# Leading small matmuls, wider fillers, masks through an ACT copy, and a re-searched order in an attention and mixer kernel

## The chip, the cores and the metric

The kernel runs on one core of a Trainium2 chip. The metric is the device time of one execution in microseconds (us), median of several executions; lower is better. The profile's span is 1.7 us shorter than the device time of the same execution (170.1 against 171.84 in the profile of the kernel before), so the two are compared only with their own kind. Engines are called PE (matmuls), DVE (vector), ACT (scalar), POOL and SP.

## The reference

A gated recurrent attention of 4 batches, 8 heads, 768 positions, head size 48, then a token mixer and a channel mixer.

```python
# attention, per batch and head
for t in range(S):
    state = alpha[t][:, None] * state + outer(k[t], v[t])
    y[t] = q[t] @ state
x = y.transpose(0, 2, 1, 3).reshape(B, S, H * D)        # (4, 768, 384)
# mixer
h  = relu(x^T @ w_tok1) @ w_tok2                        # 768 -> 256 -> 768
u  = x + h^T
h2 = relu(u @ w_ch1) @ w_ch2                            # 384 -> 1536 -> 384
return u + h2                                           # fp32
```

## The kernel before

The kernel cuts the positions of each batch into three groups of 256, twelve groups in all; groups 0 to 2 are batch 0. For each group it forms cumulated gates ("cum"), their exponentials, scaled keys and queries ("kk", "qq"), transposes of both ("trk", "trq", evicted by "evk", "evq"), the scores of two halves ("G0", "G1"), their causal masks ("mask0", "mask1"), the state updates (the K product "K", additions "sa", multiplications "sm"), the output of the group itself ("y"), and two rounds of matmuls that add the state's part ("ia", "ib", with a small copy between them as a fence). Evictions "x" then give the mixer its input.

Three properties matter here.

First, every engine works its instructions in the order of a long list, found by a search that ran against a small model of the chip. A token such as `G0_2t` means scores of half 0 of group 2 on PE; a token that ends in `n` is left out.

```python
ENGINES = {"t": "PE", "s": "ACT", "v": "DVE", "g": "POOL", "y": "SP", "n": "NONE"}
ORDER = """
f2cumw_0n f1trq_1t f1trq_0t f2cumw_1t f1trk_1n f1trk_0n ...
... K1t E2s G0_1t mask0_1v IE2s ldw_wt10g Et2s y0t ia0t
f2y_2n fe0s f2trk_2t ib0t f1trk_2t x0_0s f2G0_2n x1_0s ld_qt2y qq2g trq2t ld_kt2y f0trk_2t kk2v sa0_1v sm0_1g
ld_vt2y trk2t f0y_1t y1t ldw_wt20g evk2v evq2s sa1_1v sm1_1g f0G0_2t G0_2t mask0_2v ld_at3y f1K_2t f0G1_2t vb2s
ia1t K2t sa0_2v G1_2t P3g sm0_2g ldw_wc10g t1_0_1_0t ... mask1_2v cum3t E3s ib1t ... y2t ia2t x0_1v fe2v ib2t ...
"""                                                      # ... marks cuts
```

Second, PE's granted clock falls to half in places. In the profile of the kernel before it is 0.50 from 23.34 to 26.75 us, 3.41 us, behind a wait of PE of 1.58 us. The model has a rule of its own for this clock. Against the half clock the list holds optional fillers, matmuls on a zero tile into a PSUM bank that is about to be used:

```python
def fill(nm, bank, sizes=(1, 2, 4)):                     # groups 0 to 2 only
    return [O(f"f{j}{nm}_", {"PE": pe([384] * z)["PE"], "NONE": (0.0, 0.0)}, -100, writes=[bank],
              mm=z, emit=lambda e, z=z: g.fill(bank, z)) for j, z in enumerate(sizes)]
```

Third, the model takes PE's instructions to come in blocks, and lets PE wait where a block is late. The profile of before shows 19 packets of 16 KB on PE's instruction queue for 2461 matmuls and as many weight loads, and one wait of PE for issue, behind matmul 351; that such a wait is one for a block is the model's assumption. The place where it lets one block end and the next begin is called an edge here. The model counts matmuls (two instructions each), asks for the next block when it crosses an edge, and expects it `fetch(s)` ns later:

```python
count, edge, fetched = 0.0, 95.0, 0.0
...
while edge < count + o.mm:
    cross = st + occ * (edge - count) / o.mm
    late = max(0.0, fetched - cross)
    occ, lat = occ + late, lat + late
    fetched = cross + late + fetch(st)
    edge += 127.5

def fetch(s):
    return 4300.0 if s < 20000.0 else 5000.0 if s < 60000.0 else 4300.0 if s < 82000.0 else 3300.0
```

A mask multiplies 1024 scores per partition, read from PSUM in f32, by a bf16 triangle, and writes bf16:

```python
masks.append(O(f"mask{sl}_", dve(1024), 12 + sl, writes=[gtm], reads=[gp], preds=[G],
               emit=lambda e, sl=sl, gp=gp: g.mask(gtm, gp, sl)))
```

## Time and profile before

| what | kernel before |
|---|---|
| device time, median of the first 3 timed runs | 170.48 us (170.17 to 170.59) |
| the profiled execution | 171.84 us, span 170.1 us, mean clock 0.99 |
| PE busy | 163.0 us, 96% of the span |
| half clock inside the work | 23.3 to 26.8 us |
| hand-over: end of the second state matmuls of group 2 | 28.45 us |
| saturated stretch: hand-over to the start of the last matmul | 138.18 us |
| tail after it | 3.49 us |

The last three rows add up to the span: 28.45 + 138.18 + 3.49 = 170.12 us. I use this cut throughout: before the hand-over PE waits for loads and for batch 0's attention, after it PE is never short of work. The list of what PE waited for says how short the first part's list of suspects is (the columns are microseconds in total, number of times, longest):

```profile
PE ps L675 <- issue: 1.6, 1, 1.6
PE ps L675 <- DVE zs L604: 1.1, 1, 1.1
```

The second line is the start of the kernel. The first is a wait for nothing but the instruction itself, and it is the only one of its kind.

### The profile page before, as it was taken

The numbers are of one execution on the slowest core, as the hardware profiler recorded it, in microseconds if no ns is written. First come the engines' busy times: TensorE is split into PE (matmuls) and PEld (weight loads), VectorE is DVE, ScalarE is ACT, GpSimd is POOL, SyncE is SP. The second block draws the span as 40 slices with busy tenths as digits, with TensorE's granted clock in tenths as the row PEclk, the third lists the DMA queues.
The fourth block names the chain that finished last, engine by engine and source line by source line (L and its number), as shares of the span: only waits on it lengthen the run. The fifth ranks groups of instructions, "written<-read, shape, count | busy, mean of one in ns | idle before, by whom it ended". The sixth has DMA issues, their size and how long they took to land.

```text
span 170.1 us, 5655 instructions
## 1 busy us (share of the span) xinstructions
PE 163.0 (96%) x2461; PEld 104.5 (61%) x2461; DVE 118.3 (70%) x209; ACT 81.8 (48%) x160; POOL 60.2 (35%) x69
## 2 busy tenths in 40 slices
PE   7899969999999999999999999999999999999992
PEld 3476635676666666666666766766665666665661
DVE  4279837787869778989798897898653647573151
ACT  3868644755884637278637651666412313141000
POOL 5047637430830132929869939600200000000000
PEclk9999978999999999999999999999999999999999
DMA  5999999999999386999949200010003000110343
GB/s 137 322 321 320 228 248 294 229 271 270 252 216 286 103 227 204 323 329 258 291 152 272 101 2 0 4 50 4 0 4 139 0 4 2 46 46 4 115 177 125
DMA packets 57369, 27.10 MB, mean 159 GB/s; under 512 B 50432, under 2 KB 57344, under 8 KB 57344
## 3 DMA queue, kind: packets, MB, share of 16 engines
q1 hardware_dynamic: 53232, 23.34, 48.6%
q0 software_dynamic: 3824, 3.15, 11.9%
q8 instruction: 19, 0.31, 0.7%
q10 hardware_dynamic: 288, 0.26, 0.4%
q14 instruction: 6, 0.05, 0.1%
HBM read 25.17 MB, written 4.72 MB: 176 GB/s over the span
## 4 chain that ended last, share of the span: by engine, by line
PE 92%; DMA 2%; DVE 2%; issue 1%; ACT 1%; DVEq 0%
PE ps L889 28%; PE ps L894 28%; PE ps L675 18%; PE ps L870 5%; PE ps L863 4%; PE ps L737 3%; PE ps L881 2%; DMA at<-in_alpha_dram 2%; PE ps L741 2%; PE ps L868 1%; DVE pkk L722 1%; DVE pkq L722 1%; ACT la L669 1%; ACT IE L706 0%; DVE x L779 0%
## 5 line engine op out<-in xcount | busy, mean ns | idle before, releaser
L894 PE MATMUL ps<-wc,rt 128*128 128x384 bf16 (+2 forms) x300 | 52.3, 320 | 0.0
L889 PE MATMUL ps<-ut,wc 128*128 128x384 bf16 x288 | 51.5, 326 | 0.0
L858 ACT ACTIVATE rt<-ps 128x384 bf16<-128x384 f32 x55 | 25.7, 492 | 30.4 <-PE ps L889 30.2
L894 PEld LDWEIGHTS <-rt 128*128 128x128 bf16 x300 | 27.8, 98 | 16.4
L889 PEld LDWEIGHTS <-wc 128*128 128x128 bf16 x288 | 27.1, 98 | 17.1
L791 DVE TENSOR_TENSOR gtm<-ps,mk 128x1024 bf16<-128x1024 f32 x24 | 28.7, 1217 | 3.1 <-PE ps L675 2.7
L860 DVE TENSOR_SCALAR rt<-ps 128x384 bf16<-128x384 f32 x41 | 21.5, 550 | 6.0 <-PE ps L889 5.9
L898 DVE TENSOR_TENSOR o<-ps,u 128x384 f32<-128x384 f32 (+2 forms) x25 | 13.2, 535 | 11.1 <-PE ps L894 9.1
L820 POOL TENSOR_TENSOR ss<-tmp,E 128x192 bf16<-128x192 f32 x13 | 6.6, 507 | 26.6 <-DVE tmp L817 26.1
L722 POOL TENSOR_TENSOR pkq<-qt,E 128x768 bf16<-128x768 f32 x7 | 12.7, 1813 | 6.2 <-PE ps L863 5.2
L675 PE MATMUL ps<-zs 128*128 128x384 bf16 x50 | 12.8, 382 | 1.1 <-DVE zs L604 1.1
L722 POOL TENSOR_TENSOR pkk<-kt,IE 128x768 bf16<-128x768 f32 x6 | 10.9, 1814 | 7.7 <-DVE kt L714 4.4
L778 ACT COPY tpq<-ps 128x1024 bf16<-128x1024 bf16 x8 | 10.5, 1313 | 5.0 <-PE ps L737 3.9
L874 DVE TENSOR_TENSOR u<-ps,x 128x384 bf16<-128x384 f32 x18 | 9.3, 551 | 3.7 <-PE ps L870 3.5
L718 POOL TENSOR_TENSOR qt<-qt,lf 128x384 f32<-128x384 f32 x8 | 8.0, 998 | 8.1 <-ACT lf L672 8.1
L675 PE MATMUL ps<-tpq,tpk 48*64 48x128 bf16 x384 | 8.9, 222 | 1.6 <-issue 1.6
L870 PE MATMUL ps<-ht,wt 128*128 128x384 bf16 x48 | 10.3, 326 | 0.0
L817 DVE TENSOR_TENSOR tmp<-ps,ss 128x192 f32<-128x192 f32 x16 | 5.7, 355 | 5.2 <-PE ps L675 3.9
L863 PE MATMUL ps<-x,wt 128*128 128x384 bf16 x48 | 9.2, 340 | 0.0
L722 DVE TENSOR_TENSOR pkk<-kt,IE 128x768 bf16<-128x768 f32 x6 | 5.7, 954 | 4.7 <-ACT IE L706 4.4
L675 PEld LDWEIGHTS <-tpk 48*64 48x64 bf16 x384 | 6.4, 109 | 3.1 <-issue 2.4
L779 DVE CAST x<-ps 128x384 bf16<-128x384 f32 x12 | 6.4, 554 | 2.7 <-PE ps L675 2.4
(85 smaller groups left out, 208.5 us busy)
## 6 DMA issues: line engine op xcount, KB each, us to landing
at<-in_alpha_dram SPq DMA_DIRECT2D x12, 384.0 KB, 6.2
kt<-in_k_dram SPq DMA_DIRECT2D x12, 384.0 KB, 5.1
qt<-in_q_dram SPq DMA_DIRECT2D x12, 384.0 KB, 6.0
vt<-in_v_dram SPq DMA_DIRECT2D x12, 384.0 KB, 5.7
out_dram<-o SPq DMA_DIRECT2D x22, 192.0 KB, 2.1
wc<-in_moe_w_ch_dram POOLq DMA_DIRECT2D x3, 384.0 KB, 7.7
wc<-in_moe_w_ch_dram POOLq DMA_DIRECT2D x2, 576.0 KB, 8.7
wt<-in_moe_w_tok_dram POOLq DMA_DIRECT2D x2, 384.0 KB, 6.5
```

The source lines that it names most:

```text
L675: return self.pe.matmul(out, lhsT=lhsT, rhs=rhs, start=start, stop=stop, skip_group_check=True)
L722: self.shared(self.eng[e].tensor_tensor(self.t(dst)[:, :, :, 0:D], self.t(src).rearrange("p h s d -> p s h d"), bass.AP(tensor=f.tensor, o ...
L778: return self.act.copy(d, s)
L791: self.nc.vector.tensor_tensor(self.t(gtm)[:, sl, :, :], self.pair(gp).rearrange("p a (j t) -> p (a j) t", t=128), bass.AP(tensor=m.tensor ...
L858: self.act.activation(d, s, AF.Relu)
L860: self.nc.vector.tensor_scalar_max(d, s, 0.0)
L863: self.pe.matmul(self.bank(bank)[:, 0:HD], lhsT=self.wt1[:, kc, m * 128 : m * 128 + 128], rhs=self.t(x), start=(kc == 0), stop=(kc == NS - 1))
L870: self.pe.matmul(self.bank(bank)[:, 0:HD], lhsT=self.wt2[:, kc, i * 128 : i * 128 + 128], rhs=self.t(hts[kc]), start=(kc == 0 and not x), ...
L874: self.nc.vector.tensor_tensor(self.t(u), self.bank(bank)[:, 0:HD], self.t(x), ALU.add)
L889: self.pe.matmul(self.bank(bank)[:, 0:HD], lhsT=self.wc1[:, kc, mc * 128 : mc * 128 + 128], rhs=self.t(ut)[:, kc, half * 384 : half * 384 ...
L894: self.pe.matmul(self.bank(bank)[:, 0 : c1 - c0], lhsT=self.t(rts[mc][0])[:, i * 128 : i * 128 + 128], rhs=self.wc2[:, mc, c0:c1], start=( ...
L898: self.nc.vector.tensor_tensor(self.t(o)[:, c0:c1], self.bank(bank)[:, 0 : c1 - c0], self.t(u)[:, c0:c1], ALU.add)
```

## The change

The intent was fourfold: 64 matmuls of 64 columns ahead of all others, meant to start PE's clock with little data and to shift the block edges; fewer and wider fillers, meant to hold the clock with fewer instructions; masks split so that ACT shares DVE's load in batch 0; and a new search with the model's `fetch` taken as 6.3 us, instead of 4.3 to 5.0, between 12.5 and 30 us. (In the trace of before 6.3 us pass from the crossing of edge 222, at 16.8 us, to the end of the issue wait, at 23.11.) The core of the diff (the order list, which is replaced as a whole, is cut):

```diff
 def fetch(s):
-    return 4300.0 if s < 20000.0 else 5000.0 if s < 60000.0 else 4300.0 if s < 82000.0 else 3300.0
+    return (2300.0 if s < 4000.0 else 4500.0 if s < 12500.0 else 6300.0 if s < 30000.0 else 5300.0 if s < 60000.0 else
+            4400.0 if s < 82000.0 else 3400.0)
...
-FULL = (0, 1, 2, 3, 4, 5)
+FULL = (0, 1, 2)
+COPIED = (0, 1, 2)
...
-        def fill(nm, bank, sizes=(1, 2, 4)):
+        def fill(nm, bank, sizes=(1, 2, 3)):
...
-            return [O(f"f{j}{nm}_", {"PE": pe([384] * z)["PE"], "NONE": (0.0, 0.0)}, -100, writes=[bank],
+            return [O(f"f{j}{nm}_", {"PE": pe([512] * z)["PE"], "NONE": (0.0, 0.0)}, -100, writes=[bank],
...
+            if sl and n in COPIED:
+                go = O("gc", act(1024), 11.5, writes=[gtm], reads=[gp], preds=[G],
+                       emit=lambda e, gp=gp: g.gcopy(gtm, gp))
+                masks.append(O(f"mask{sl}_", dve(1024, True), 12 + sl, writes=[gtm], port=True, preds=[go],
+                               emit=lambda e, sl=sl: g.mask2(e, gtm, sl)))
+                continue
...
+    for z in (16, 32, 64):
+        bank = V("one")
+        P.op(f"pad{z}_", {"PE": pe([64] * z)["PE"], "NONE": (0.0, 0.0)}, -99000.0, writes=[bank], mm=z,
+             emit=lambda e, z=z, bank=bank: g.pad(bank, z))
...
-ORDER (906 tokens)
+ORDER (912 tokens)
+
+    def gcopy(self, gtm, gp):
+        self.act.copy(self.t(gtm)[:, 1], self.pair(gp).rearrange("p a (j t) -> p (a j) t", t=128))
```

`FULL` also matters: groups 3 to 5 now transpose in 16 half-height matmuls each instead of 8 full ones.

## The prediction

> **What bounds the kernel now.** I read the page's engine table and slices first, then the PE timeline and clock of the first 35 us, then who PE waited for.
>
> ```profile
> PE 163.0 (96%) x2461; PEld 104.5 (61%) x2461; DVE 118.3 (70%) x209; ACT 81.8 (48%) x160; POOL 60.2 (35%) x69
> PE   7899969999999999999999999999999999999992
> PEclk9999978999999999999999999999999999999999
> ```
>
> PE is busy in 96% of the span, so the sum of PE work sets the end. But 50 of its matmuls are fillers on a zero tile (line 675, 12.8 us busy), all in the first 25 us, and only there do the PE and clock rows dip. The 5 us windows, PE only (length, busy, count, clock, DMA share, GB/s):
>
> ```profile
> 15.00:20.00 5.00, 5.00 (x143) 1.00 1.19 240
> 20.00:25.00 5.00, 3.42 (x83) 0.83 1.14 270
> 25.00:30.00 5.00, 4.62 (x99) 0.82 1.14 282
> 30.00:40.00 10.00, 9.98 (x115) 1.00 1.20 250
> ```
>
> The kernel has two stages. Before about 28.5 us PE waits for loads and for the chain of batch 0's attention; fillers hide that. After it PE never stops until 167.2 us, and 2.9 us of tail (last addition, last store) follow. A clock of 0.83 and 0.82 over two windows means 0.17 x 5 / 0.5 + 0.18 x 5 / 0.5 = 3.5 us at half clock. Why, the PE timeline shows (start, length, instruction, idle before and who ended it):
>
> ```profile
> 20.91 0.34 PE L675 MATMUL ps<-zs 128*128 128x384 bf16 x1
> 21.17 0.36 PE L675 MATMUL ps<-tpq,tpk 48*64 48x128 bf16 x12
> 23.11 0.25 PE L675 MATMUL ps<-tpq,tpk 48*64 48x128 bf16 x4 [1.58 <-issue]
> ...
> 25.63 1.36 PE L863 MATMUL ps<-x,wt 128*128 128x384 bf16 x4
> ...
> 28.25 0.27 PE L675 MATMUL ps<-ss,tpq 48*128 48x48 bf16 x8 [0.31 <-DVE junkDVE L779]
> 28.45 1.47 PE L863 MATMUL ps<-x,wt 128*128 128x384 bf16 x8
> ```
>
> A group of 16 scores stops after 12 for 1.58 us with nothing to wait for but its own issue. Counting in the trace, this is after matmul 351; a matmul is two instructions, and the plan in the kernel puts block edges at 95, 222.5 and 350 matmuls. One 16 KB packet of the instruction queue ran at 20.65 to 21.53 us, while edge 222 had been crossed at 16.8[...]. The stall and the cold clock delay the last scores, their mask, and so the first point from which PE is full: the end of group 2's last state matmuls at 28.5 us. I call it the **hand-over**.
>
> [...] 384-wide matmuls start every 320 ns until 6.1 us, then every 163, and every 320 again in the 3.5 us after the stall. [...]
>
> **The change, part by part.**
>
> *Fillers and small matmuls.* 15 fillers of 512 columns instead of 50 of 384, and 64 zero matmuls of 64 columns first. From the rate of cold 384-wide ones (320 ns), a 64-wide takes 53 ns: 64 take 3.4 us, from 1.1 to 4.5, before the first real matmul at 5.2. They cost no time, count 64 matmuls, and so move the first block edge to the transposes of group 0 (about 8.6 us instead of 11.8). PE's instructions grow by 77 matmuls: +64, -35, +48 for transposes.
>
> *Half transposes.* Groups 3 to 5 go from 8 wide transposes (8 x 56 = 0.447 us) to 16 small ones in pairs. An island of 48 small ones between two wide groups costs 0.90 us in the trace of before; less 0.2 for entry and exit, 0.23 per 16. Six times 0.447 - 0.23 is **1.3 us saved**. But the searched order has 50 changes between wide, score and state forms after the hand-over against 45, at 0.1 to 0.15 us each: **0.5 to 0.75 us lost**. The list of operations after the hand-over is the same 326 otherwise. Net -0.6 us.
>
> *Masks and order of batch 0.* Three masks move: ACT copies 1024 elements out of PSUM (1.0 us, as its plain 1024-wide copies)[...]. Group 1's k and group 2's q multiplication go from POOL (1.81 each) to DVE (0.95). So DVE becomes the chain. Worked by hand with the durations of before, loads landing as before at 3.7 us plus 1.22 us each by place: q and k of group 0 7.6 to 9.4; query eviction (1.31) to 10.7; q and k of group 1 to 12.5; first mask to 13.7; key eviction to 14.3; wait for the K product (v lands as eighth load, 12.3, and POOL's cast waits for DVE's port turn), two states to 15.3; mask to 16.5; two bf16 masks to 17.7, so y of group 0 at 17.2 (before: 17.1); group 2's q waits for exponentials that ACT now makes after two copies, 17.9 to 18.8; k to 19.7; states with a POOL step between to 20.9; two x to 21.9; query eviction to 23.2; state and x to 24.0; mask to 25.2; state to 25.5; bf16 mask to 26.1; y of group 2, state matmuls, fence, state matmuls: hand-over at **27.1 us**. Up to it both orders have done the same 4 token matmuls, so nothing else is owed. Operations overlap by some 0.07 us in the trace, which I rounded in only partly: 26.6 to 27.1.
>
> *Block edges.* Up to y of group 1 the new order has 350 matmuls. Edge 222 falls at about 14.4 us, plus 6.3 is 20.7. y of group 1 could run at 19, so it stops there for 1 to 1.7 us, but its successor on the chain, the key transposes of group 2, only has to be evicted by 23.2, when the query eviction ends. The stall is still there, now in slack. The next edge, 477, lies at the hand-over itself: 20.7 + 6.3 = 27.0, nearly no wait.
>
> Sum: hand-over 28.5 to about 26.9 = -1.6, later work -0.6, tail unchanged: 170.5 - 2.2 = 168.3. I take **168.2 us**.
>
> **Rivals.** (a) *Cold at the hand-over.* PE from 19.9 to 23.3 has some 1.5 us of work in 3.4, as before at that place (the 20 to 25 us window: 3.42 of 5 busy). If the clock halves there, PE needs 2 x 2 us for scores, fillers, K product and token matmuls, and y of group 2 comes 0.8 us later; if it halves one window later, saturated work loses 1.7 us. For: only 15 fillers, and before went cold with more. Against: the cold window would mostly end at 26.75 as before. Time: 169 to 170.2.
> (b) *The fetch stall was the whole chain.* Without stall and cold clock, before's own order would hand over near 25.7 (scores done at 22.8 rather than 25.7). If the search kept that and my DVE chain is pessimistic by its rounding and waits, hand-over 25.5: 166.5 to 167. Against: DVE's sum alone, about 16.8 us from 7.6 on with overlaps, gives 24.4 with no wait at all.
> (c) *A transfer takes its place.* By the first channel matmuls (35.5 before, about 34 after) DMA must bring 12 + 6 loads, two token weights and one or two channel weights, 24 to 26 units of 393 KB; before brought about 28 by 36.0. The second channel weight, issued after the first, would land near 35, where it is wanted near 35.5. Up to 1 us of idle PE: 169.2.
> (d) *Denser small matmuls later.* My count of edges gives one interval of 3.4 us near 94 us, where before's shortest was 4.3 us[...]. 0.5 us or less.
>
> **Range and chances.** (a), (c) and (d) together add up to 2 us and can hardly take more than the gain; (b) takes off 1.7. Range 166.2 to 169.9. Over 2% faster means below 167.1, so (b) in full with little of the others: 0.22. Slower by over 2% would need a new cold stretch or stall of 5 us: 0.03. Within 2%: 0.75.
>
> **What would show it.** Right: in the profile after, fillers x15, the small zero matmuls end before 5 us; the issue stall of 1 us or more sits in y of group 1, not in the scores; DVE is nearly gap-free from 7.6 to 26 us[...]; the second state matmuls of group 2 end at 26.5 to 27.2; PE has no idle time over 0.3 us from there to the last matmul, and that stretch is about 138 us against 138.7. Wrong: a hand-over earlier than 26 (DVE was not the chain, or fewer waits), a half clock after 26.8, idle PE before a channel matmul for a weight, issue waits after 30 us, or a saturated stretch that isn't 0.3 to 1 us shorter.

Passages are cut from this text that told of the hardware what no trace of this case shows. Among them is the author's figure for a bf16 mask, a term of the hand chain; the chain's times stay as they were put on record. The sum comes to what it came to then: hand-over -1.6, later work -0.6, so 170.5 - 2.2 = 168.3, taken as 168.2 us. But the 27.1 us of the chain rest in part on the term that is cut, and no trace of before showed it: its masks take 1217 ns (L791), and the bf16 masks of the changed kernel then took 681 (L819). Four notes:

- The 6.3 us in the steps on block edges are measured in the trace of before, 23.11 - 16.8. That a block is asked for when an edge is crossed is an assumption.
- A window in rival (a) is a stretch of 3.41 us, as long as the half clock of that trace. The size of rival (d), 0.5 us or less, is the author's estimate and was not shown.
- The cost of a change of form is in the trace of before: behind a wide matmul the first small one starts after 256 ns, where the next wide one starts after 162, and behind the last score a wide one starts after 148 ns, where scores follow each other after 14.
- The first nine loads of before land at 4.26 to 14.08 us, 1.23 us apart on average; the eighth lands at 12.88, where the prediction has 12.3.

## The result, and the profile after

The changed kernel took **171.00 us** in the median of 4 runs (170.76 to 171.21), beside 170.32 us (170.16 to 170.59) for the kernel before on the same chip. The ratio is 1.0038 with an interval from 1.0016 to 1.006: the same, within 2%, and outside the predicted range of 166.2 to 169.9 us. Ratios here are the mean time of one kernel's fast runs over that of the other's in the same rounds, so they are not quite the ratio of the medians quoted.

The profiled execution was the longest of the four, 171.21 us, span 169.5. From the page of the changed kernel, the engine table's first line and the slices of PE and of its clock:

```profile
PE 160.4 (95%) x2538; PEld 103.9 (61%) x2538; DVE 109.3 (64%) x194; ACT 90.1 (53%) x178; POOL 60.2 (36%) x69
PE   7795799999999999999999999999999999999991
PEclk9999759999999999999999999999999999999999
```

PE does 2.6 us less work, DVE 9 us less, ACT 8 us more. The clock dips in two neighbouring slices, as before, but one slice earlier and deeper (7 and 5 tenths, where before had 7 and 8). The windows of the changed kernel, PE only (length, busy, count, clock, DMA share, GB/s):

```profile
15.00:20.00 5.00, 2.90 (x132) 0.90 1.06 282
20.00:25.00 5.00, 4.96 (x94) 0.50 1.24 250
25.00:30.00 5.00, 4.74 (x95) 0.92 1.14 256
```

PE had 2.1 us of idle time from 15 to 20 us and then ran at half clock until 25.8 us, twice as long as before. The PE timeline of the changed kernel (start, length, instruction, idle before and who ended it):

```profile
1.12 3.59 PE L690 MATMUL ps<-zs 128*128 128x64 bf16 x64 [1.12 <-DVE zs L619]
17.56 0.75 PE L690 MATMUL ps<-vb,gtm 64*128 64x48 bf16 x32 [1.20 <-ACT gtm L815]
20.24 0.82 PE L690 MATMUL ps<-vb,gtm 64*128 64x48 bf16 x32
23.60 1.07 PE L690 MATMUL ps<-tpq,tpk 48*64 48x128 bf16 x32
24.61 1.03 PE L690 MATMUL ps<-zs 128*128 128x512 bf16 x2
25.57 0.52 PE L690 MATMUL ps<-vb,pkk 64*64 64x48 bf16 x16
27.04 0.66 PE L690 MATMUL ps<-vb,gtm 64*128 64x48 bf16 x32
28.26 1.64 PE L891 MATMUL ps<-x,wt 128*128 128x384 bf16 x8
```

The lines are the small matmuls, y of groups 0 and 1, the scores of group 2, two fillers, the K product of group 2, its y, and the token matmuls at the **hand-over, 28.26 us**. No wait for issue is left, neither in the scores nor elsewhere; the list of PE's waits in the changed kernel starts with ACT:

```profile
PE ps L690 <- ACT gtm L815: 1.8, 2, 1.2
PE ps L690 <- ACT la L684: 1.4, 2, 1.0
```

The new waits are for the copies that ACT now makes ahead of y of group 0. And DVE, which I had made the chain (timeline of the changed kernel):

```profile
24.30 1.22 DVE L810 TENSOR_TENSOR gtm<-ps,mk 128x1024 bf16<-128x1024 f32 x1
26.14 0.36 DVE L845 TENSOR_TENSOR tmp<-ps,ss 128x192 f32<-128x192 f32 x1 [0.61 <-PE ps L690]
26.41 0.68 DVE L819 TENSOR_TENSOR gtm<-gtm,mk 128x1024 bf16<-128x1024 bf16 x1
```

It waits 0.61 us for the K product, which stood on PE behind the scores and two fillers. At the other end of the kernel the last additions wait for an output buffer that an earlier store still holds (DVE timeline of the changed kernel):

```profile
165.78 0.62 DVE L926 TENSOR_TENSOR o<-ps,u 128x256 f32<-128x256 f32 x2 [1.28 <-DMA out_dram<-o]
```

In the kernel before such a wait is there too, 2.02 us, but it ends at 161.97 us, and the last additions wait for PE alone:

```profile
161.97 1.07 DVE L898 TENSOR_TENSOR o<-ps,u 128x384 f32<-128x384 f32 x2 [2.02 <-DMA out_dram<-o]
166.89 0.29 DVE L898 TENSOR_TENSOR o<-ps,u 128x128 f32<-128x128 f32 x1 [0.24 <-PE ps L894]
```

In the three parts, the two profiles differ so:

| part | before, this profile | after, this profile | difference |
|---|---|---|---|
| hand-over | 28.45 | 28.26 | -0.19 |
| saturated stretch | 138.18 | 137.41 | -0.77 |
| tail | 3.49 | 3.83 | +0.34 |
| span | 170.1 | 169.5 | -0.6 |

So profile against profile the change is 0.6 us faster, while the timed medians say 0.7 us slower. Both readings are correct: the profiled execution of before was a long one of its kind. The experiments begin there.

### The profile page after: what moved, and what is told of

It is laid out like the page before. It is cut to its first block, busy times and chain, and to the rows that moved or that the text cites. A ratio compares the mean times of both kernels' runs of the same rounds, so it can differ in the third digit from the quotient of the medians.

```text
span 169.5 us, 5838 instructions
## 1 busy us (share of the span) xinstructions
PE 160.4 (95%) x2538; PEld 103.9 (61%) x2538; DVE 109.3 (64%) x194; ACT 90.1 (53%) x178; POOL 60.2 (36%) x69
## 4 chain that ended last, share of the span: by engine, by line
PE 82%; DMA 6%; SPq 3%; DVE 3%; issue 2%; ACT 1%; POOL 0%; DVEq 0%; POOLq 0%; ACTq 0%
PE ps L917 28%; PE ps L922 25%; PE ps L690 13%; PE ps L891 5%; PE ps L898 5%; DMA at<-in_alpha_dram 3%; SPq L651 3%; PE ps L760 3%; PE ps L909 2%; DMA out_dram<-o 2%; DVE gtm L819 1%; ACT gtm L815 1%; PE ps L896 1%; DVE o L926 1%; DVE pkk L741 1%
## 5 line engine op out<-in xcount | busy, mean ns | idle before, releaser
L886 ACT ACTIVATE rt<-ps 128x384 bf16<-128x384 f32 x67 | 30.9, 492 | 27.4 <-PE ps L917 27.0
L917 PEld LDWEIGHTS <-wc 128*128 128x128 bf16 x288 | 27.0, 98 | 17.5
L888 DVE TENSOR_SCALAR rt<-ps 128x384 bf16<-128x384 f32 x29 | 15.5, 551 | 10.6 <-PE ps L917 10.4
L848 POOL TENSOR_TENSOR ss<-tmp,E 128x192 bf16<-128x192 f32 x11 | 5.6, 507 | 24.5 <-DVE tmp L845 24.4
L675 POOL TENSOR_TENSOR at<-at 128x384 f32<-128x384 f32 x8 | 8.0, 994 | 9.4 <-DVE vb L798 5.4
L797 ACT COPY ut<-ps 128x768 bf16<-128x768 bf16 x6 | 4.8, 800 | 10.2 <-PE ps L909 10.2
L690 PE MATMUL ps<-zs 128*128 128x64 bf16 (+1 forms) x79 | 8.5, 280 | 1.2 <-DVE zs L619 1.1
L733 POOL TENSOR_TENSOR kt<-kt,at 128x384 f32<-128x384 f32 x7 | 7.0, 993 | 6.8 <-DVE pkk L741 5.0
L741 DVE TENSOR_TENSOR pkq<-qt,E 128x768 bf16<-128x768 f32 x7 | 6.7, 952 | 4.0 <-ACT E L725 3.9
L798 DVE COPY tpq<-ps 128x1024 bf16<-128x1024 bf16 x6 | 7.8, 1304 | 2.0 <-PE ps L760 1.2
L741 POOL TENSOR_TENSOR pkq<-qt,E 128x768 bf16<-128x768 f32 x5 | 9.0, 1812 | 0.1
L798 POOL CAST vb<-vt 128x768 bf16<-128x768 f32 x6 | 4.9, 822 | 11.0 <-DVE tpk L798 10.8
```

What stands on the lines that cost most here:

```text
L690: return self.pe.matmul(out, lhsT=lhsT, rhs=rhs, start=start, stop=stop, skip_group_check=True)
L741: self.shared(self.eng[e].tensor_tensor(self.t(dst)[:, :, :, 0:D], self.t(src).rearrange("p h s d -> p s h d"), bass.AP(tensor=f.tensor, o ...
L798: return self.shared(self.eng[e].tensor_copy(d, s))
L886: self.act.activation(d, s, AF.Relu)
L888: self.nc.vector.tensor_scalar_max(d, s, 0.0)
L917: self.pe.matmul(self.bank(bank)[:, 0:HD], lhsT=self.wc1[:, kc, mc * 128 : mc * 128 + 128], rhs=self.t(ut)[:, kc, half * 384 : half * 384 ...
```

## The experiments

All outputs are right. Each table row below is read from the run's profile; "half clock" is the time at half clock inside the work, and "profiled us" the device time of the profiled execution. Medians are of the timed runs.

| run | hand-over | half clock, us | stretch | profiled us | median us | ratio to before |
|---|---|---|---|---|---|---|
| before, first profile | 28.45 | 3.4 | 138.18 | 171.84 | 170.32 | |
| after | 28.26 | 6.8 | 137.41 | 171.21 | 171.00 | 1.0038 |
| before_again | 28.96 | 10.2 | 139.97 | 174.12 | 171.69 | 1.0055 |
| before_look | 27.57 | 3.4 | 138.17 | 170.93 | one run | |
| after_again | 28.22 | 6.8 | 137.24 | 171.25 | 170.94 | 0.9992 |
| after_warm | 28.70 | 0 | 137.83 | 171.72 | 171.73 | 1.0068 |
| after_nopad | 30.09 | 13.7 | 139.67 | 174.94 | 174.02 | 1.0128 |
| before_half | 28.78 | 6.8 | 140.48 | 174.44 | 173.67 | 1.0143 |
| after_swap | 27.92 | 3.4 | 137.75 | 170.87 | 171.01 | 0.9957 |
| order_b | 29.25 | 3.4 + 6.8 | 139.65 | 174.07 | 173.74 | 1.011 |
| after_nocopy | 29.60 | 6.8 | 139.20 | 173.97 | 173.93 | 1.0121 |
| before_wide | 26.85 | 3.4 at 97.7 | 141.50 | 173.53 | 173.19 | 1.0134 |
| before_wide2 | 27.81 | 3.4 + 3.4 | 141.82 | 174.84 | 175.33 | 1.0225 |
| after_lean | 28.59 | 10.2 | 138.37 | 172.13 | 171.65 | 1.003 |
| before_realign | 26.59 | 0 | 138.40 | 170.18 | 170.19 | 0.9965 |
| mix | 29.26 | 3.4 at 30.2 | 138.96 | 173.47 | 172.73 | 1.0101 |
| realign_2 | 25.96 | 0 | 138.46 | 169.61 | 170.31 | 0.9977 |
| mix_nopad | 26.61 | 3.4 at 28.7 | 142.24 | 174.03 | 174.54 | 1.02 |

The profiles of before_again, after_nopad and before_half fell in runs counted as slow; no time is concluded from them. Three theories were tested. *Base*: the profile that the prediction started from was not typical, and the gain of 1.6 us was not there to be had. *Clock*: the half clock from 19.0 to 25.8 us holds the changed kernel's hand-over back. *Chain*: the order of DVE and PE in group 2 does.

### before_again and before_look: the same code, timed again

No edit.

> The kernel before, unchanged, profiled once more. The profiled execution of before took 171.84 us, its timed ones 170.2 to 170.6; so far the profile shows 1.4 us that the timed runs need not have. Theory 1 (the profile I predicted from was a long execution): the executions here lie at 170.2 to 170.6 with spans of 168.5 to 168.9, the hand-over (end of the second state matmuls of group 2) comes at 26.8 to 27.4 instead of 28.5, and the issue wait in the scores of group 2 is shorter than 1.0 us or the half-clock window lies elsewhere; the stretch from the hand-over to the last matmul is 138.2 as in the first profile. Rival (profiling itself lengthens before, for all executions alike): again 171.5 or more with the same 1.6 us issue wait at 21.5.

> The kernel before once more, one look. Its executions so far: 168.7 to 168.9 us of span at a mean clock of 0.997 to 1.0, 169.2 to 170.1 at 0.99, 171 to 174 at 0.97 to 0.98; the two profiles (0.99 and 0.97) have the same 1.5 us issue wait at 21.4, followed by 3.4 and 10.2 us at half clock. If this profile has a clock near 1.0: the issue wait is the same 1.5 us, there is no half-clock stretch before the last matmul, hand-over at 26.9 to 27.3, span about 168.8. If it is slow again: issue wait the same, half clock 6.8 us or more.

The first gave a ratio of 1.0055 (1.002 to 1.0091) for identical code. That alone makes 1.0038 a size that this comparison can't tell from nothing. In its profile the issue wait is the same:

```profile
PE ps L675 <- issue: 1.5, 1, 1.5
```

but the windows of before_again show how differently the clock answered:

```profile
25.00:30.00 5.00, 4.74 (x91) 0.50 1.12 253
30.00:35.00 5.00, 5.00 (x28) 0.68 1.19 229
```

The half clock lasted 10.2 us, 4.2 of them after the hand-over, where every lost matmul is lost for good: 4.2 / 2 = 2.1 us, and 139.97 - 2.1 = 137.9 us is the usual stretch again. In before_look the wait was 1.46 us and the half clock 3.4. The kernel before was executed 57 times, from 169.63 to 175.74 us, mean 171.56. Of the 53 with a recorded clock, 23 had 0.995 or more and took 170.63 us on average, 18 had 0.985 to 0.995 and took 171.48, 12 had less and took 173.8 (169.63 to 171.88, 170.91 to 171.79, 172.55 to 175.74). The first profile of before, 171.84 us at 0.99, belongs to the middle class; the timed runs of 170.17 to 170.59 sit where the first class does, though their clocks weren't recorded. The wait was 1.46 to 1.58 us in all three profiles of this code; what followed from it was not the same. In before_look the wait ended at 22.63 us instead of 23.11, as the 16 KB packet of PE's instruction queue ahead of it ended at 21.08 instead of 21.53, and the half clock lay at 24.4 to 27.8 us instead of 23.3 to 26.8; with the same stretch, 138.17 us, nearly the whole difference of 0.91 us between these two executions (0.88) lies ahead of the hand-over. The theory's own numbers were missed (170.2 to 170.6 us, a hand-over at 26.8 to 27.4), and before_again alone looked like its rival, that profiling lengthens every execution; but before_look was profiled too, and its 170.93 us lie below the median of the runs beside it, 171.68. So the base theory is supported; no profile of before at full clock was caught.

### after_again: the changed kernel again, five rounds

No edit.

> The kernel after, unchanged, in five more rounds beside the kernel before. Reading so far: before's executions fall into groups by granted clock (span 168.5 to 168.9 at 0.997 to 1.0, 169.2 to 170.1 at 0.99, 171 to 174 at 0.97 to 0.98), after's first four all lie at 168.9 to 169.5 although their clock is 0.976 to 0.987. If that reading holds, after's six executions here stay within 170.5 to 171.5 us, before's spread over 170.2 to 174 or more, and the median of before is the higher one if more than half of its executions are below clock 0.995. If after's first four were a lucky draw: after spreads as before does.

170.94 us in the median (170.10 to 171.25), ratio 0.9992 (0.9952 to 1.0032): the 0.4% of the first comparison did not come back. Its profile has the hand-over at 28.22, again after 6.8 us of half clock, but not by the same path. The half clock lay at 17.5 to 24.3 us, 1.5 us earlier; PE timeline of after_again:

```profile
25.18 0.43 PE L690 MATMUL ps<-vb,pkk 64*64 64x48 bf16 x16
26.56 0.71 PE L690 MATMUL ps<-vb,gtm 64*128 64x48 bf16 x32
27.52 0.24 PE L690 MATMUL ps<-ss,tpq 48*128 48x48 bf16 x5 [0.20 <-issue]
```

The K product began 0.39 us sooner than in the first profile, DVE didn't wait for it, and y of group 2 began 0.48 us sooner. Then PE stopped for 0.20 us for issue, after three of the eight first state matmuls: at matmul 479, 6.3 us after the edge at matmul 351 was crossed (21.26 us) and 1.5 us after the end of a 16 KB packet of PE's instruction queue (26.05). The ten runs of the changed kernel have a standard deviation of 0.35 us, the 57 of the kernel before 1.39 us. Had the changed kernel the same share of long runs as before (12 of 53), ten in a row without one would come with a chance of (41/53)^10 = 0.08, so a narrower spread is likely but not shown.

### after_warm: does the half clock hold the hand-over back?

```diff
- E2s y0t              ... y1t ia1t           ... f1G0_2t ib1t           ... f1K_2t f0K_2n K2t
+ E2s f1y_0t f2y_0t y0t ... y1t f2trk_2t ia1t ... f1G0_2t f2G0_2t ib1t   ... f1K_2t f0K_2t f2K_2t K2t
```

These add 15 fillers of 512 columns in the holes of the changed order (2553 matmuls instead of 2538). The text on record says 13, as it counts 3 ahead of group 1's second state matmuls; the edit makes them 5.

> The kernel after, with more 512-wide fillers on the idle places of batch 0: 5 ahead of y of group 0, 3 between y of group 1 and its first state matmuls, 3 instead of 2 ahead of group 1's second state matmuls, 6 instead of 2 ahead of the K product of group 2 (13 matmuls more). Theory 1 (the 6.8 us at half clock from 19.0 to 25.8 cost the new order 0.9 to 1.1 us against my hand chain): clock 1.0 from 5.3 us on, hand-over at 27.0 to 27.4 instead of 28.3, time 0.7 to 1.2 us less than after, so 169.8 to 170.3. Rival (the chain through DVE, ACT and POOL sets the hand-over, and the clock only fills slack): clock up, hand-over at 28.0 or later, time within 0.3 us of after's 171.0. Third outcome: the fillers bring back an issue wait at block edge 350 or 477, seen as such.

The clock was full all the way (0.997 to 1.0), and the time did not fall: 171.73 us, ratio 1.0068 (1.0047 to 1.0089), hand-over 28.70. The PE timeline of after_warm says why:

```profile
24.70 1.47 PE L687 MATMUL ps<-zs 128*128 128x512 bf16 x6
26.10 0.43 PE L687 MATMUL ps<-vb,pkk 64*64 64x48 bf16 x16
28.70 1.48 PE L888 MATMUL ps<-x,wt 128*128 128x384 bf16 x7
```

The scores start 0.5 us later than in the changed kernel (24.13), behind five fillers, and six warm fillers then hold PE for 1.4 us where two cold ones had held it for 1.0. So the K product comes at 26.10 instead of 25.57 us, and DVE waits 0.58 us for it where it had waited 0.61. The clock theory falls in the form I gave it: removing the half clock with fillers buys nothing here, where the fillers ahead of the scores and of the K product stand in the chain themselves.

### after_nopad: the small matmuls taken away

```diff
- ld_qt0y pad64_t f1G1_2n
+ ld_qt0y pad64_n f1G1_2n
```

> The kernel after without the 64 small zero matmuls ahead of all others; nothing else changed. All block edges fall 64 matmuls later: edge 95 in the second exponent sum or the transposes of group 1, edge 222 in the K product or y of group 0 near 18, edge 350 in the scores or K product of group 2 near 23.7. If the small matmuls are what keeps issue waits away[...]: an issue wait near edge 350, 0.3 to 1.5 us[...]; time 0.5 to 2 us more than after. If they do nothing: no issue wait over 0.2 us, time within 0.3 us of after.

174.02 us (172.27 to 175.52), ratio 1.0128. PE, which first waits until 5.2 us, stays cold until 9.5 us: from 5 to 10 us it runs 36 matmuls in 4.85 us of busy time, where the changed kernel, at full clock from 5.35 us, runs 47 in 4.26. It goes to half clock again from 19.7 to 33.4 us, and issue waits of 0.43 and 0.55 us appear at matmuls 351 and 862, where the first profile of the changed kernel has none. In the changed order the small matmuls earn their place twice over: with them the clock is full 4 us earlier, and these two waits are gone. This run can't divide its loss between the two.

### before_half: half transposes alone, in the old order

```diff
-FULL = (0, 1, 2, 3, 4, 5)
+FULL = (0, 1, 2)
```

> The kernel before with one part of the change alone: groups 3 to 5 use half transposes (16 small in place of 8 wide), order unchanged. My prediction's step: 0.447 - 0.23 = 0.22 us saved per group of transposes, six of them, 1.3 us, less 0.1 to 0.15 us for entry and exit at each isolated one; in before's order all six stand alone between wide groups but for one, so net 0.1 to 0.7 us saved. Rival: entry and exit eat it all, 0 +- 0.2 us. Block edges after the hand-over move by 8 matmuls per transpose group, which could make an issue wait.

173.67 us, ratio 1.0143 (1.005 to 1.0237). The saving expected for this part is not seen. PE now waits for the eviction of a query transpose; in the code half transposes take a pair of PSUM banks where full ones take one, which fits these waits. The PE timeline of before_half:

```profile
47.03 0.41 PE L741 MATMUL ps<-idn,pkk 64*128 64x64 bf16 x16 [0.80 <-ACT tpq L778]
```

A second such wait, 0.32 us, follows at 57.4 us, one of 0.16 us for DVE comes between them, and the clock fell for 6.8 us in this profile, 2.0 of them after the hand-over. An estimate from these numbers: 140.48 - 0.80 - 0.32 - 0.16 - 2.0 / 2 = 138.2 us, the stretch of before (138.18). So nothing was saved, as the rival says. The traces show why: from the start of the last wide matmul ahead of a transpose to the second wide one behind it, an isolated group of 16 half ones took 258 + 340 + 173 = 771 ns, and the 8 full ones of before 163 + 446 + 163 = 772.

### after_swap: one swap on DVE

```diff
- r13s sa0_2v E3s t1_0_0_0t t1_0_0_1t t1_0_0_2t t1_0_0_3t mask1_2v
+ r13s mask1_2v sa0_2v E3s t1_0_0_0t t1_0_0_1t t1_0_0_2t t1_0_0_3t
```

The bf16 mask of group 2 no longer stands behind the state addition that waits for the K product.

> The kernel after with one exchange on VectorE: the last bf16 mask of group 2 goes ahead of the addition of group 2's state, which in the profile of after waits 0.61 us for the K product (behind two fillers on a PE at half clock). Theory 1 now (after's hand-over is set by the chain through VectorE and its neighbours, not by the clock): mask from 25.7 to 26.4, y of group 2 at 26.4 to 26.6, hand-over 27.6 to 27.9 instead of 28.3, time 0.3 to 0.7 us less than after (170.3 to 170.7). Rival (clock): hand-over stays at 28.1 or later, time as after.

y of group 2 starts 0.7 us sooner, but the hand-over gains 0.3 us only. The PE timeline of after_swap:

```profile
26.33 0.61 PE L687 MATMUL ps<-vb,gtm 64*128 64x48 bf16 x32
26.78 0.69 PE L687 MATMUL ps<-ss,tpq 48*128 48x48 bf16 x8
```

The first state matmuls now take 0.69 us instead of 0.26. The second of them waits for the new state, which DVE finishes at 26.99 us, and 0.17 us more pass at matmul 479, the edge that also held after_again up. Two chains, the mask's (26.33) and the state's, end within 0.7 us of each other. The swap isn't the only difference, though: the half clock of this profile lasted 3.4 us instead of 6.8, and the K product began at 24.95. In after_again, without the swap, y began at 26.56, so that the swap's own part in the 0.7 us may be as small as 0.2. The timed median, 171.01 us, can't be told from the changed kernel's.

### order_b: group 2's transposes and scores moved up

The key transposes, y of group 1 and the scores of group 2 were moved ahead of other work, fillers of that stretch dropped, and the mask swap kept (some 25 tokens move).

> The kernel after with the order of group 2 changed further: its query eviction on ScalarE right after its transposes, its key transposes ahead of y of group 1 and its key eviction on VectorE, the fence of group 1 ahead of a logarithm that waits for GpSimd, its scores as soon as both evictions are done, its first mask ahead of two states, no fillers ahead of scores and K product, y ahead of the first token matmuls. By the same kind of hand chain: scores at 21.5 to 22 instead of 23.6, first mask done at 23.7 to 24.2, second at 24.5 to 25.3, y at 24.6 to 25.4. If theory 1 holds and nothing else binds: hand-over at 26 to 27, time 1.2 to 2.2 us less than after (168.8 to 169.8). What may take its place: the first token weight, landed at 24.5 in after; the weight piece of channels 0 to 511, landed at 36.7 in after where its first matmul started at 37.0, so PE idles ahead of that one for up to 1.5 us; a half clock in the saturated part, since PE has fewer fillers (each 3.4 us of it costs up to 1.7).

A miss: 173.74 us. The scores came 1.3 us sooner (22.28 us), but the PE timeline of order_b shows y of group 2 stopping after two matmuls:

```profile
25.08 0.23 PE L687 MATMUL ps<-vb,gtm 64*128 64x48 bf16 x2
26.68 0.78 PE L687 MATMUL ps<-vb,gtm 64*128 64x48 bf16 x30 [1.37 <-DVE gtm L816]
```

The bf16 mask itself waited 0.64 us for an operation of POOL: the program makes it take turns with POOL's operations (the reason in the code reads "shared port"), and doesn't for the masks that read f32 from PSUM. With that idle time the clock was at half from 25.0 to 31.9 us, 2.6 us of it after the hand-over. PE also waited 0.97 us for issue at matmul 1758 (100.43 us). Without these the stretch would be 139.65 - 0.97 - 2.6 / 2 = 137.4 us, as in the changed kernel.

### after_nocopy: the masks back on DVE

```diff
-COPIED = (0, 1, 2)
+COPIED = ()
```

The three copies leave the order.

> The kernel after with the three copied masks taken back (second masks of groups 0 to 2 read f32 from PSUM on VectorE as before, three ScalarE copies gone), order else unchanged. The bf16 masks take 0.68 us here against 1.22: if VectorE's chain sets the hand-over, the two masks of groups 0 and 1 add 1.1 us less what they waited for the copies (y of group 0 waits for the second copy), and group 2's adds 0.5: hand-over 0.6 to 1.3 us later, time 0.6 to 1.3 us more than after. If the ScalarE copy was itself the wait: no change or faster by up to 0.4.

173.93 us, hand-over 29.60, 1.3 us later than the changed kernel's. PE's largest wait in after_nocopy:

```profile
PE ps L687 <- DVE gtm L807: 2.4, 2, 1.8
```

In the changed order the copies are worth these 1.3 us of hand-over. The rest of the loss is no part of this: the stretch grew by 1.8 us, of which 0.57 is an issue wait at matmul 1758 (100.28 us) and 0.44 a wait for ACT at 33.3 us. The copies are not a gain over the kernel before, whose own order never needed them.

### before_wide and before_wide2: wide fillers alone, in the old order

```diff
- sizes=(1, 2, 4) ... pe([384] * z)
+ sizes=(1, 2, 3) ... pe([512] * z)
- f2cumw_0n f1trq_1t f1trq_0t
+ f2cumw_0n f1trq_1n f1trq_0t
```

41 fillers of 512 columns stand for 50 of 384. before_wide2 also drops `f1K_2` and `f0G1_2`.

> The kernel before with the part wider fillers alone: 512 columns, sizes 1, 2, 3, one pair of the first fillers dropped so that the cold ones still end by 4.6 us; order else unchanged. 41 fillers instead of 50, 9 matmuls fewer ahead of block edge 350, which then lies in the state matmuls of group 1 after the scores of group 2. Theory (the wait is tied to a block edge, 127.5 matmuls apart[...]): edge 222 crossed near 16.9, the issue wait moves from the second half of the first scores of group 2 to those state matmuls, at 22.2 to 23.1, and shrinks to 0.5 to 1.0 us; the first mask of group 2 starts near 21.9 instead of 23.4. Executions with clock over 0.995: span 167.7 to 168.5. If the wait has nothing to do with edges: same place, same 1.5 us.

> As before_wide, and without the three fillers between the first scores of group 2 and the state matmuls that follow (they are behind the block edge, on the path to the second scores). If the path after the issue wait sets the hand-over: second scores 0.4 to 0.6 us earlier than in before_wide (1 us at half clock), span 0.3 to 0.6 us less where the clock stays over 0.995. If PE then goes to half clock more often: clock 0.98 or less in most executions and span 169.5 or more.

Both were slower, and before_wide is the run that taught most. Its PE timeline:

```profile
23.16 0.25 PE L673 MATMUL ps<-ss,tpq 48*128 48x48 bf16 x6 [0.45 <-issue]
97.17 0.23 PE L673 MATMUL ps<-vb,gtm 64*128 64x48 bf16 x5 [1.65 <-issue]
```

The wait still lies at matmul 351, and it still ends near 23.1 us as in before (23.11). But with nine filler matmuls fewer, all 16 scores lie ahead of that edge, their mask isn't held, the wait shrinks to 0.45 us, the clock stays up, and the hand-over comes at 26.85 us. Then the same shift moves a later edge, at matmul 1630, into dense small matmuls: a new wait of 1.65 us at 95.5 us, and a half clock of 3.4 us behind it. Against the first profile of before the hand-over is 1.6 us earlier; 1.65 us of wait and 3.4 / 2 = 1.7 us of half clock are lost in the middle, through nothing but the count. before_wide2 lost the clock once more, at 23.8 us.

### after_lean: two fillers fewer ahead of the K product

```diff
- G1_2t f1K_2t f0K_2n K2t
+ G1_2t f1K_2n f0K_2n K2t
```

> The kernel after without the two fillers ahead of the K product of group 2. In after they ran from 24.6 to 25.6 at half clock, the K product and the addition of group 2's state behind them, and the bf16 mask behind that. If they are on the path to the hand-over: K product at 24.6 to 24.9, mask from 25.7, y of group 2 at 26.3 to 26.6, hand-over 27.5 to 27.8, time 0.4 to 0.7 us less than after. If they are what brings the clock back at 25.8: half clock until 29.2, hand-over 27.8 or later, and up to 1.5 us more than after.

171.65 us (171.03 to 174.47), ratio 1.003. In this profile the K product began at 24.70 us and DVE didn't wait for it, but the half clock lasted 10.2 us instead of 6.8 and reached past the hand-over; at half clock the four token matmuls ahead of y took until 27.07. So here one was traded for the other. That these fillers end the half clock isn't shown: two other runs, 171.03 and 171.17 us, had mean clocks of 0.987 and 0.98, as the changed kernel has. An issue wait of 0.65 us came up at matmul 1758 (98.46 us).

### before_realign and realign_2: wide fillers and nine small matmuls

The order of before_wide, with nine zero matmuls of 64 columns ahead of `cum3`, so that every later edge lies again where it lay in before.

```diff
+    for z in (9,): ... g.pad(bank, z)
- mask1_2v cum3t
+ mask1_2v pad9_t cum3t
```

> before_wide plus 9 matmuls of 64 columns on a zero tile ahead of the first exponent sum of group 3, where PE waited 0.46 us for ScalarE. They make good the 9 matmuls that the wider fillers took out, so that every block edge from 477 on lies again on the operations on which it lies in before, while edge 350 stays after the first scores of group 2. Theory (an issue wait belongs to a block edge, at a fixed matmul index, and costs by what stands there): wait of 0.4 to 1.2 us at matmul 351 as in before_wide; the wait of 1.65 us at matmul 1630 (95.5 us) is gone; hand-over 26.8 to 27.4, from there to the last matmul 138.2 as in before instead of 141.5; span 168.3 to 169.0 (170.0 to 170.7 us) in the executions at full clock, 2.5 to 3.3 us less than before_wide. Rival (the wait at 95 us came of something else in before_wide): still there, time 172.6 or more.

> Identical to before_realign, beside mix_nopad on the same chip. If its narrow spread (169.97 to 170.97 in six runs, clock 0.997 or more) is a property of the order and not luck: six runs within 1.2 us, median 170.0 to 170.8, again no issue wait behind the hand-over and a wait of 0.3 to 0.6 us at index 351. If it was luck: some runs at a clock below 0.99 and over 171.5 us, as with the kernel before.

170.19 us (169.97 to 170.97), and again on another chip 170.31 (169.61 to 170.87). The new wait in the middle is gone in both, and all twelve runs had a clock of 0.997 or more. PE timeline of before_realign:

```profile
22.45 0.20 PE L677 MATMUL ps<-ss,tpq 48*128 48x48 bf16 x2
23.18 0.25 PE L677 MATMUL ps<-ss,tpq 48*128 48x48 bf16 x6 [0.54 <-issue]
26.59 1.47 PE L869 MATMUL ps<-x,wt 128*128 128x384 bf16 x8
```

In realign_2, against what I had expected, the wait at matmul 351 was not there at all; the same eight matmuls run through (PE timeline of realign_2):

```profile
22.32 0.27 PE L677 MATMUL ps<-ss,tpq 48*128 48x48 bf16 x8
25.96 1.31 PE L869 MATMUL ps<-x,wt 128*128 128x384 bf16 x7
```

So PE could go on at 22.4 us in that execution, and only near 23.1 in the others: this time varies too. The 16 KB packet on the instruction queue ahead of it ended at 20.89 us here, at 21.66 in before_realign. The hand-over came 0.63 us earlier for a wait of 0.54 us less. The medians of this version lie below the changed kernel's two (171.00, 170.94) and below before's beside it (171.49, 170.91); the intervals, 0.9919 to 1.0011 and 0.9939 to 1.0016, still reach 1. Its medians are the lowest of all versions, by a fraction of a percent that isn't shown to be real; that none of its twelve runs was long may be part of it.

### mix and mix_nopad: the early hand-over with the changed order behind it

before_wide's order up to the hand-over, the changed kernel's order after it; mix has two pads of 20 and 18 small matmuls besides, mix_nopad has none.

> A try for a version that beats both: the order of before_wide up to the hand-over (no copied masks), after's order with half transposes behind it, and 38 small matmuls (20 ahead of the exponent sum, 18 ahead of the last state matmuls) so that after's block edges fall on the operations for which its order was searched. If the parts add up: hand-over 26.9 to 27.6, stretch 137.3 to 137.8 as in after, span 167.7 to 168.9 (169.4 to 170.6 us), below after's 170.9 and below before's full-clock mean of 170.8. If after's order needs its own first part (transfers, buffers): PE waits for a weight or a PSUM bank after 30 us and the time is 171 or more.

> The order of before_wide up to the hand-over, the changed kernel's order behind it (with its half transposes), without the two pads of the run called mix, in which a fetch edge fell on the second pad. Counted in matmuls, no two edges after the hand-over are closer than 4.5 us here, so no issue wait over 0.3 us behind the hand-over; the wait at index 351 stays, 0.2 to 0.5 us. If the two orders' advantages add up: hand-over 26.6 to 27.0 us (as before_wide and before_realign), saturated stretch 137.4 to 138.0 us (as the changed kernel), span 167.7 to 168.7, 169.4 to 170.4 us, all at a clock of 0.99 or more. If the changed order's shorter stretch needs its own starting state (its queues and buffers at the hand-over), waits on DVE, ACT or loads appear in the first 10 us after it and the stretch is 138.5 or more: 170.5 to 171.5 us.

Both missed, each by a new wait. In mix an edge fell on the pad itself, and PE stood 2.3 us at 26.5 us. In mix_nopad the hand-over came at 26.61 us, as hoped, and PE stopped four matmuls later (PE timeline of mix_nopad):

```profile
29.06 1.44 PE L888 MATMUL ps<-x,wt 128*128 128x384 bf16 x4 [1.55 <-ACT x L794]
```

The eviction that it needs stood on ACT behind two logarithms, and the first of these had waited 1.75 us for a product on POOL, which in this prefix comes later than in the changed kernel's. With that wait (1.55), the half clock behind it (3.4 / 2 = 1.7) and a wait of 1.08 us for an output buffer at 155.7 taken off, the stretch is 142.24 - 4.33 = 137.9 us, near the changed kernel's. So the shorter stretch seems to be the new order's own, but the two halves of an order can't be joined at will.

## Why the prediction was wrong, step by step

The predicted time, 168.2 us, lies 3.01 us under the profiled execution of the changed kernel. The terms below make it up, to the rounding: 0.08 for rounding 168.28 to 168.2, then four sizes.

**The base: 1.36 us.** The step "hand-over 28.5 to about 26.9 = -1.6 ... 170.5 - 2.2" failed. It measured a gain in a profile of 171.84 us and took it from a median of 170.48. The profile held 3.4 us of half clock, which the runs behind this median, by their times, hardly had; their clocks weren't recorded, so this is inferred. Taking 1.71 us, 138.18 and 3.49 from the median of 170.32 leaves a hand-over of 26.9 us for a fast execution of before, an estimate from those three numbers. before_look (27.57 with a half clock that late) and the class means, 170.63 against 171.48 us, point the same way. Most of the predicted gain was already there in the runs that it was to be taken from.

**The hand-over of the changed kernel: 1.41 us.** The step "state to 25.5; bf16 mask to 26.1 ... hand-over at 27.1", and the further rounding to 26.9, failed in its last quarter. Up to the first mask of group 2 the chain by hand held to 0.4 us: y of group 0 at 17.56 instead of 17.2, the query eviction ending at 23.54 instead of 23.2, the mask starting at 24.30 instead of 24.0. Then the state addition started at 26.14, waiting 0.61 us for the K product. I had written that "nothing else is owed" on PE; the fillers ahead of the K product were. The bf16 mask behind it ended at 27.09 instead of 26.1, and the first state matmuls, the fence and the second took until 28.26, 1.17 us instead of 1.0. That is the first profile. In after_again the K product was in time, the mask ended at 26.66, and the hand-over came at 28.22 all the same: the steps behind the mask took 1.56 us, with an issue wait of 0.20 us in the state matmuls, at the very edge of which I had written "nearly no wait". So what failed in both is the last part of the chain, which has no room for PE's own delays; which delay fills it, fillers at half clock or the issue wait, changed from one execution to the next. That DVE alone was the chain was too simple: after_swap shows a state chain 0.66 us behind the mask's.

**Rival (a), cold at the hand-over,** came true as an event, 6.8 us of half clock, and not as the cause I had given it: after_warm took the half clock away and the hand-over moved from 28.26 to 28.70. But its fillers lengthened the chain in the same step, and no run removed both the half clock and the fillers. How much of the 1.4 us the half clock is worth without fillers stays open.

**Rival (b), the wait as the whole chain,** was right for the old order and not for the new one. I had put the hand-over of before's order without stall and cold clock near 25.7 us; realign_2, where neither happened, reached 25.96, and before_realign, with 0.54 us of wait, 26.59. The changed order left that chain for one of its own that was 1.7 to 2.3 us longer.

**The issue wait in y of group 1** did not happen: the step "so it stops there for 1 to 1.7 us" failed. y began at 20.24 us instead of 19, and its matmul 351 ran at 20.73 us without a wait. The 16 KB packet ahead of it on the instruction queue had ended at 19.09 us, and each of the 17 issue waits in these profiles ended 1.35 to 1.58 us after such a packet. By these numbers a wait there would have ended at 20.4 to 20.7 us (an estimate), so y came just as it would have been over. The part of the change that meant to remove the issue wait did so in the first profile; in the second 0.20 us were left, one edge later.

**The saturated stretch: 0.17 us the other way.** Predicted 0.6 us shorter, in a range of 0.3 to 1; measured 0.77. (The prediction counted to the end of the last matmul, 138.7 us in before; the cut here is its start, 138.18.) The sum was right, and the trace bears its parts out. Two of the six half transposes stand alone (29.83 and 33.47 us) and save nothing, as in before_half. The pair at 40.96 us saves 0.22 us together, and those at 50.06 and 52.66 us, beside other small matmuls, some 0.22 each: 0.65 us in all, an estimate from start-to-start times.

**The tail: 0.34 us.** "Tail unchanged" failed. The last additions waited 1.28 us for an output buffer, but that this is the cause is not shown: after_again has a tail of 4.0 us, and there the profile puts the wait at the same place (1.46 us) down to PE. No range of mine had a place for it.

**Rivals (c) and (d)** did not happen: no wait for a weight and no issue wait after 30 us in the profiles of the changed kernel. Rival (d) came close: the edge that it meant was crossed at 94.31 us, and matmul 1758 ran without a wait at 97.14. In order_b, after_nocopy and after_lean PE waited 0.57 to 0.97 us at that matmul. Right, too, were the 15 fillers and the small matmuls ending at 4.7 us. The bf16 mask took 0.68 us, the masks that read f32 from PSUM 1.22.

The range was too narrow, since its low and high ends were both hung on one profile of before. The class that I gave the highest chance, within 2%, is the one that came.

What the change did do: it exchanged an issue wait of 1.5 us followed by a half clock of varying length for a longer chain with at most 0.2 us of issue wait and a half clock that, in both profiles, ended before it could cost saturated work. Its mean over ten runs is 170.87 us, that of before over 57 is 171.56; the fast runs compared round by round are the same.

## What to carry to other kernels

Before a gain is taken from a time, check that the profile it was read from is an execution of that time; here 1.4 us of a 2.2 us gain was the difference between two executions of the same code. Filler work on an engine isn't free when the next link of the chain stands behind it (15 more fillers in after_warm: hand-over 28.70 us instead of 28.26), and the count of instructions is itself a resource: in before_wide nine matmuls fewer decided which work an issue wait held up, near the edit (0.45 us at matmul 351 instead of 1.58) and far from it (1.65 us at matmul 1630, where before had none). A part of a searched order is not worth the same in another order, so judge it there or together.

## What the runs showed of issue waits and of the half clock

- PE waited 0.2 (after_again) to 2.3 us (mix) for issue at single places, where it waited at all at the same matmul for a given order (351 in all three profiles of before, 1630 in before_wide and before_wide2), and a half clock could follow. All 17 issue waits of 0.2 us or more in these profiles ended 1.35 to 1.58 us after a 16 KB packet of PE's instruction queue had ended. Where PE waited between 22 and 29 us, the wait ended 5.9 to 6.5 us after the edge before it was crossed; no trace shows a request.
- The half clock came back in the midst of the work, after one wait of 1.58 us in the first profile of before, and of 1.65 us in before_wide. The same code, with a wait of 1.46 to 1.58 us each time, showed half clocks of 3.4 us (the first profile of before, before_look) and 10.2 us (before_again), and the twelve of its 53 runs at a mean clock under 0.985 are its twelve slowest, 172.55 to 175.74 us. Stretches came as 3.4, 6.8, 10.2 and 13.7 us.
- Work meant to hold the clock cost as much as the cold clock here: 15 more fillers took the half clock from 6.8 us to 0 and the hand-over from 28.26 to 28.70 us (after, after_warm).
